# One product of each expert layer by seven products of quarters, with sums accumulated in PSUM

## The chip, the cores and the metric

The kernel runs on one core of a Trainium2 chip. The metric is the device time of one execution in microseconds; the median of three runs counts.

## What is computed

The reference is an attention block followed by a mixture of experts. The first half gives, for 8 batches and 8 heads of 576 positions and width 64, a softmax over the scores that lie within tau of the row's maximum, times v. Its output is 4608 token rows of 512 numbers. The second half sends each token to one of 8 experts by a hash of its id:

```python
expert_idx = token_ids * np.int64(2654435761) % np.int64(E)
for e in range(E):
    mask = expert_idx == e
    xe = x[mask]
    h = np.maximum(xe @ w1[e], 0.0)
    out[mask] = h @ w2[e]
```

w1[e] is 512 x 1024, w2[e] is 1024 x 512; all is fp32.

## The kernel before

**Stages.** The attention stage takes about the first half of the time. While it runs, the tokens are ranked by expert, and x is written to a scratch tensor in DRAM (x_scratch). The experts follow, in the order of their token counts, 0 to 7. The slots of an expert are 544 (expert 0), 576 (1 to 4) or 600 (5 to 7); slots beyond that go to a loop for the overflow, which has nothing to do here. Expert 0's first layer is done plainly during attention's end (`early_h`, `late_h`); the change does not touch it.

**One expert.** All operands stand transposed: h = relu(w1^T x) has features on the partitions and tokens as columns. A layer is one matrix product a b, where a is the weight (the stationary operand) and b the activations (the moving one). Both are cut into 2 x 2 blocks, and the four blocks of the result are made by seven products in Winograd's form, not eight (`seven`, L926): with sums s2, s3, s4 (and s1, in place of a21) of the blocks of a, and t2, t3, t4 (and t1, in place of b12) of those of b,

- p1 = a11 b11, and c11 = p1 + a12 b21
- u2 = p1 + s2 t2, u3 = u2 + s3 t3, c21 = u3 + a22 t4
- k5 = s1 t1, u4 = u2 + k5, c22 = u3 + k5, c12 = u4 + s4 b22

A product is 2 output blocks of 128 features by n_k chunks of 128 inner elements, with half the tokens as columns (272, 288 or 300; 240 in expert 7's second layer, whose last 120 slots `last_tile` does, L983). In layer 1 n_k is 2, and the block of a is done in two groups of columns, so it has 14 products of 4 matmuls (`layer1`, L963); in layer 2 n_k is 4 and there are 7 products of 8 matmuls (`layer2`, L972). Each product has a PSUM tile of its own; four tiles go round (`bank2`, L851, tiles sc and bank2). Each of the sums u2, u3, u4 and each output block is an add on DVE (L861) from PSUM to SBUF; p1 is copied by ACT (L951), and in layer 1 ACT applies relu to each output block (L948).

**Weights of layer 2.** For experts 0 to 6 the columns of w2 are dealt: output feature 4 m + i is row m of block i (`dealt`, L877; `w2_blocks`, L880). So a weight load from w_sb in layer 2 takes every fourth word of a row; one from the sums w2_s takes every second. Expert 7 takes them as they stand. The dealt order lets DVE transpose the output in 32 x 32 squares (`put_squares`, L1024), which POOL then scatters to the output in DRAM (L1036).

**The order of the work.** Both expert blocks are under `manual_schedule`: the engines run what the code emits, in that order. `seven` calls a function after each step (`side1` in layer 1, `side2` in layer 2), which emits the work for what comes next. In layer 1 of expert e these are the sums of w2 (`sums_w2`), the second half of the previous expert's squares, the first half of the sums of h, and the squares of the next expert's x (`turn_x`, L1052, with 16 transfers xT<-xq on SP's queue, L1064). In layer 2 they are the sums of the next expert's w1 and x, the gathers of x for expert e + 2 (`fetch`, on POOL), the load of w1 for expert e + 2 (on SP), and the first half of the squares. For expert 0 all of the next expert's x is turned in its layer 2.

Of the kernel before, what the change touches and what calls it, by code (L numbers as in the profile page):

```python
# [20 lines left out]
def kernel(  # L21
# [805 lines left out]
    with tc.tile_pool(name="m_x", bufs=1) as m_x, \  # L827
         tc.tile_pool(name="m_o", bufs=3) as m_o, \
         tc.tile_pool(name="m_s", bufs=1) as m_s:
# [7 lines left out]
        nc.gpsimd.memset(oT[:, :, CAP:SL], 0.0)  # L837
        o_end = m_x.tile([P, DIN], FP32, name="o_end")
        mark = m_x.tile([P, 1], FP32, name="mark")
# [4 lines left out]
        h_s = m_s.tile([P, 3, FH, CH], FP32, name="h_s")  # L844
        halves = [m_s.tile([P, 2, CH], FP32, name=n) for n in ("p1", "u2", "u3", "u4")]
        CHL = 32 * (NB - 4) // 2

        ps_m = ctx.enter_context(tc.tile_pool(name="ps_m", bufs=2, space=PSUM))
        turn = [0]

        def bank2():  # L851
            turn[0] ^= 1
            if turn[0]:
                return ps_sc.tile([P, 2, 512], FP32, name="sc")
            return ps_m.tile([P, 2, 512], FP32, name="bank2")

# [52 lines left out]
        def sums_w2(e):  # L909
            s1 = None  # L910
            if e == E - 1:
                spare = w_pool.tile([P, CO, F], FP32, name="w1_sb")
                s1 = w_tiles["s1"] = spare[:, :, 0:D2]
            return left(*w2_blocks(e, w_tiles[e, 2]), w2_sums(e), s1)

# [9 lines left out]

        def seven(a, a_s, b, b_s, m0, outs, relu, after):  # L926

            (a11, a12, s1, a22), (s2, s3, s4) = a, a_s
            (b11, t1, b21, b22), (t2, t3, t4) = b, b_s
            c11, c12, c21, c22 = outs  # L930
            n_k, width, dealt_out = a11.shape[1], b11.shape[2], len(a11.shape) == 4
            p1, u2, u3, u4 = (t[:, :, 0:width] for t in halves)

            def product(x, y):
                ps = bank2()
                for i in range(2):
                    c0 = m0 + P * i
                    for c in range(n_k):
                        lhsT = (x[:, c, :, i] if dealt_out else
                                x[:, c, c0:c0 + P])  # L940
                        nc.tensor.matmul(ps[:, i, 0:width], lhsT=lhsT, rhs=y[:, c],  # L941
                                         start=c == 0, stop=c == n_k - 1)
                return ps[:, :, 0:width]

            def out(c, ps, u, step):
                add(c, ps, u)()
                if relu:
                    nc.scalar.activation(c, c, AF.Relu)  # L948
                after(step)

            nc.scalar.copy(p1, product(a11, b11))  # L951
            out(c11, product(a12, b21), p1, 0)
            add(u2, product(s2, t2), p1)()
            after(1)
            add(u3, product(s3, t3), u2)()
            after(2)
            out(c21, product(a22, t4), u3, 3)
            k5 = product(s1, t1)
            add(u4, k5, u2)()
            out(c22, k5, u3, 4)  # L960
            out(c12, product(s4, b22), u4, 5)

        def layer1(e, side):  # L963

            w, half = w_tiles.pop((e, 1)), caps[e] // 2
            for g in range(NG):
                outs = [h_0[:, FH * i + 2 * g:FH * i + 2 * g + 2, half * k:half * k + half]
                        for i in range(2) for k in range(2)]
                seven(w1_blocks(w), triple(w1_s, 0, C2), x_blocks(e), triple(x_s, 0, C2, half), 2 * P * g,
                      outs, True, lambda step: side(g, step))  # L970

        def layer2(e, side):  # L972

            w, half = w_tiles[e, 2], half2(e)
            outs = [oT[:, C2 * i:C2 * i + C2, half * k:half * k + half]
                    for i in range(2) for k in range(2)]
            a = w2_blocks(e, w)
            if e == E - 1:
                a[2] = w_tiles["s1"]
            seven(a, w2_sums(e), h_blocks(0, FH, half),  # L980
                  triple(h_s, 0, FH, half), 0, outs, False, side)

        def last_tile(middle):  # L983

            w, o_sb, idx = w_tiles[E - 1, 2], o_end, gidx[:, KT - 1:KT]
            rows = CAP - 2 * CHL
            for c0, c1 in ((0, DIN - P), (DIN - P, DIN)):
                ps = bank2()
                for fo in range(FO):
                    nc.tensor.matmul(ps[0:rows, 0, 0:c1 - c0], lhsT=h_0[:, fo, 2 * CHL:CAP],  # L990
                                     rhs=w[:, fo, c0:c1], start=fo == 0, stop=fo == FO - 1)
                    if (c0, fo) == (0, FH - 1):
                        middle()
                nc.scalar.copy(o_sb[0:rows, c0:c1], ps[0:rows, 0, 0:c1 - c0])
            put_rows(o_sb[0:rows], idx[0:rows])

        def put_out(e, *groups):
# [14 lines left out]
            for tr, kts in zip(trs, groups):  # L1012
                for i, kt in enumerate(kts):
                    rows = rows_of(kt)
                    o_sb = m_o.tile([P, DIN], FP32, name="o_sb")
                    dst = o_sb[0:rows].rearrange("p (c r q) -> p r c q", c=CO, r=2)
# [52 lines left out]
        with tc.manual_schedule():  # L1069
            run(sums_w2(0), 4)  # L1070
            fill(18)
            late_h(lambda fo: (ps_sc.tile([P, 2, 512], FP32, name="sc") if fo in (2, 4) else
                               ps_m.tile([P, 2, 512], FP32, name="bank2")))
            fetch(1)
            run(sums_h(0, 0, FH), 4)

        with tc.manual_schedule():
            for e in range(E):
                more = e + 1 < E
                turns = turn_x(e + 1) if more else []  # L1080

                if e > 0:
                    w2_work, h_work = sums_w2(e), sums_h(e, 0, 2)

                    def side1(g, step):
                        if g == 0:
                            run(w2_work)
                            if step == 0:
                                put_squares(e - 1, 1)
                        else:  # L1090
                            run(h_work)
                        if step > 2:
                            run(turns, 1 if g == 0 else 2)

                    layer1(e, side1)
                    run(sums_h(e, 2, FH), 4)
                x_work = (sums_w1(e + 1) + sums_x(e + 1)) if more else []

                def side2(step):
                    if step == 0:  # L1100
                        run(turns, len(turns))
                    else:
                        run(x_work, 2)
                    if step == 2 and e + 2 < E:
                        fetch(e + 2)
                    if step == 4 and e + 2 < E:
                        load_w1(e + 2)
                    if more and step == 3:
                        put_squares(e, 0)
# [23 lines left out]
        with tc.For_i(0, n_ov, 1) as it:  # L1133
# [23 lines left out]
            for fo in range(FO):  # L1157
                nc.tensor.matmul(o_ps[:, 0], lhsT=h_0[:, fo, 0:P], rhs=w2_sb[:, fo],
                                 start=(fo == 0), stop=(fo == FO - 1))
            o_sb = m_o.tile([P, DIN], FP32, name="o_sb")  # L1160
            nc.scalar.copy(o_sb[:], o_ps[:, 0])
# [35 lines left out]
```

## Time and profile before

| | |
|---|---|
| median of three runs | 918.71 us (918.48 to 920.31) |
| the profiled execution, its own time | 931.3 us |
| its span, first to last instruction | 929.7 us |
| experts, from expert 0's second layer | 501 to 930 us |
| expert 0, layer 2, on TensorE | 501.0 to 527.0 us |
| expert 1, layers 1 and 2 | 527.0 to 583.3 us |
| expert 7, layer 1 to the last product | 861.3 to 914 us |

In a line of instructions by time: start and length in us, engine (PE is TensorE's matmuls, PEld its weight loads, DVE VectorE, ACT ScalarE, POOL GpSimd, SPq SyncE's queue), line of the kernel, operation, output<-inputs by the names of their tiles (without numbers), the shape (partitions x columns, or active rows*columns of the array and the size of the moving operand), and the count of instructions that were merged into the line. In brackets is the idle time before it and who ended that. Matmuls overlap, so a matmul's length is more than the distance to the next one's start. In a list by source the three numbers are the shortest, the median and the longest duration in ns. In a list of waits they are the sum in us, the number of waits and the longest one.

### The profile page before, as it was taken

Reading aid. Unit: us, or ns where it says so; the run is one execution under the profiler, and the core shown is the slowest. Engines: PE = TensorE matmul, PEld = TensorE weight load, DVE = VectorE, ACT = ScalarE, POOL = GpSimd, SP = SyncE. Lnnn points to the kernel's source line nnn. Section 1 sums busy time; section 2 is a strip of 40 time slices with the busy share of each in tenths; the row PEclk is TensorE's granted clock in tenths of the full one; section 3 lists DMA queues with packets and bytes.
Section 4 is the critical chain, followed back from the end, with each engine's and each line's share of the span. In section 5 each row is a group of like instructions: output and inputs, shape, how many; then the busy total and the mean of one; then the engine's idle time right before and its main releaser. Section 6 shows DMA issues by size and latency. Waiting matters only on the chain.

```text
span 929.7 us, 20725 instructions
## 1 busy us (share of the span) xinstructions
PE 909.8 (98%) x7495; PEld 662.0 (71%) x7495; DVE 757.5 (81%) x1654; ACT 457.3 (49%) x741; POOL 403.7 (43%) x528
## 2 busy tenths in 40 slices
PE   7999999999999999999999999999999999999996
PEld 4666666656666566665678888788887978878785
DVE  7999999999999999999955776767668676777551
ACT  6888888888888898888812010110201021020110
POOL 4232432456666623455423370724527073440702
PEclk9999999999999999999999999999999999999999
DMA  7354463554545668743101745364372536412101
GB/s 175 92 148 118 109 152 93 136 131 103 123 105 153 159 165 214 216 107 88 30 25 51 237 131 158 133 173 141 95 223 75 164 133 165 157 34 50 48 3 55
DMA packets 114775, 113.11 MB, mean 122 GB/s; under 512 B 32475, under 2 KB 89315, under 8 KB 114672
## 3 DMA queue, kind: packets, MB, share of 16 engines
q1 hardware_dynamic: 105168, 92.64, 37.0%
q0 software_dynamic: 9072, 18.91, 7.0%
q8 instruction: 61, 1.00, 0.4%
q14 instruction: 42, 0.34, 0.1%
q10 hardware_dynamic: 432, 0.21, 0.1%
HBM read 81.99 MB, written 21.44 MB: 111 GB/s over the span
## 4 chain that ended last, share of the span: by engine, by line
PE 65%; issue 21%; POOL 7%; DVE 3%; ACT 2%; DMA 1%; another core or an unknown queue 1%; POOLq 0%; SPq 0%; DVEq 0%; ACTq 0%
PE av L313 18%; PE sc L235 15%; PE tr L282 11%; PE sc L941 9%; PE bank L941 8%; POOL out_dram L1036 6%; PE sc L640 2%; PE av L282 1%; POOL xg L119 1%; ACT w L260 1%; DVE ns L246 1%; DVE w L271 1%; ACT wT_b L303 1%; ACT wT_a L303 0%
## 5 line engine op out<-in xcount | busy, mean ns | idle before, releaser
L260 ACT ACTIVATE w<-ns,nmx 128x576 f32<-128x576 f32 x288 | 220.5, 777 | 28.8 <-DVE ns L246 27.8
L271 DVE SCALAR_TENSOR_TENSOR w<-ns,thr,w 128x576 f32<-128x576 f32 x288 | 225.8, 816 | 0.0
L1036 POOL DMA_INDIRECT out_dram<-o_q,qidx x127 | 138.1, 1087 | 191.7 <-DVE o_q L1028 153.1
L246 DVE TENSOR_SCALAR_CACHE_REDUCE ns<-sc 128x576 f32<-128x576 f32 x288 | 205.6, 747 | 8.1 <-PE sc L235 7.4
L253 POOL TENSOR_SCALAR thr<-nmx,drop 128x2 f32<-128x2 f32 (+1 forms) x160 | 104.4, 653 | 187.3 <-DVE ns L246 177.6
L235 PE MATMUL sc<-k_sb,q 64*128 64x288 f32 (+1 forms) x1280 | 179.2, 423 | 1.0 <-DVE drop L704 0.7
L282 PEld LDWEIGHTS tr<-ident,w 64*128 64x128 f32 x2624 | 106.0, 138 | 95.4 <-ACT wT_b L303 32.4
L282 PE MATMUL tr<-ident,w 64*128 64x64 f32 x2624 | 139.5, 231 | 6.0 <-ACT wT_b L303 2.6
L948 ACT ACTIVATE h<-h 128x576 f32<-128x576 f32 (+1 forms) x56 | 38.7, 693 | 164.8 <-DVE h L861 126.1
L235 PEld LDWEIGHTS sc<-k_sb,q 64*128 64x128 f32 (+1 forms) x1280 | 93.0, 177 | 23.2 <-DVE ns L246 9.4
L313 PE MATMUL av<-wT_a,v 128*64 128x320 f32 (+1 forms) x704 | 100.6, 418 | 0.2
L303 ACT COPY wT_a<-tr 128x512 f32<-128x512 f32 (+1 forms) x128 | 81.7, 638 | 20.7 <-PE tr L282 20.2
L303 ACT COPY wT_b<-tr 128x512 f32<-128x512 f32 (+1 forms) x128 | 81.4, 636 | 17.1 <-PE tr L282 11.2
L313 PE MATMUL av<-wT_b,v 128*64 128x256 f32 x640 | 83.2, 389 | 0.0
L313 PEld LDWEIGHTS av<-wT_a,v 128*64 128x64 f32 x704 | 43.8, 137 | 29.3 <-DVE xm L352 0.7
L951 ACT COPY p<-bank 128x576 f32<-128x576 f32 (+2 forms) x11 | 7.0, 633 | 99.5 <-PE bank L941 72.5
L313 PEld LDWEIGHTS av<-wT_b,v 128*64 128x64 f32 x640 | 40.2, 136 | 18.8 <-issue 0.7
L542 POOL DMA_INDIRECT slot_scratch<-tok,slot_i x36 | 45.0, 1251 | 9.4 <-issue 7.6
L941 PE MATMUL bank<-h,w_sb 128*128 128x288 f32 (+3 forms) x192 | 48.1, 404 | 0.0
L941 PE MATMUL sc<-h,w_sb 128*128 128x288 f32 (+3 forms) x192 | 47.7, 401 | 0.0
L941 PEld LDWEIGHTS bank<-h,w_sb 128*128 128x128 f32 x192 | 46.6, 300 | 0.5
L941 PEld LDWEIGHTS sc<-h,w_sb 128*128 128x128 f32 x192 | 45.9, 289 | 0.6
(197 smaller groups left out, 1303.7 us busy)
## 6 DMA issues: line engine op xcount, KB each, us to landing
w_sb<-in_moe_w_dram SPq DMA_DIRECT2D x16, 2048.0 KB
q<-in_q_dram SPq DMA_DIRECT2D x62, 288.0 KB
v<-in_v_dram SPq DMA_DIRECT2D x32, 256.0 KB
x_scratch<-xm SPq DMA_DIRECT2D x32, 256.0 KB
xT<-xq SPq DMA_DIRECT2D x84, 80.0 KB
k_sb<-in_k_dram SPq DMA_DIRECT2D x31, 144.0 KB
k_sb<-in_k_dram SPq DMA_DIRECT2D x32, 112.0 KB
x_scratch<-xg SPq DMA_DIRECT2D x9, 256.0 KB
```

The source lines that it names most:

```text
L235: nc.tensor.matmul(sc[out_rows, i, 0:S2], lhsT=q_sb[rows, h, q0:q1], rhs=k_sb[rows, h], start=True, stop=True)
L246: nc.vector.tensor_scalar(out=ns[:].rearrange("p (i s) -> p i s", i=2), in0=sc[:, :, 0:S2], scalar1=-1.0, scalar2=None, op0=ALU.mult, op1= ...
L253: nc.gpsimd.tensor_scalar(out=thr[:, 0:j + 1], in0=stats[n][0][:, 0:j + 1], scalar1=drop[:], scalar2=None, op0=ALU.add)
L260: nc.scalar.activation(w, nss[n, j][:], AF.Exp, bias=stats[n][0][:, j:j + 1], scale=-1.0)
L271: nc.vector.scalar_tensor_tensor(out=w, in0=nss.pop((n, j))[:], scalar=stats[n][1][:, j:j + 1], in1=w, op0=ALU.is_le, op1=ALU.mult, accum_ ...
L282: nc.tensor.transpose(dst[:, r, 64 * c:64 * c + 64], src[rows, c0:c0 + P], ident[rows, rows])
L303: nc.scalar.copy(dst, tr[:, :, 0:64 * n_c].rearrange("p r (c q) -> p r c q", c=n_c))
L313: nc.tensor.matmul(av[64 * j:64 * j + 64, g, c0:c1], lhsT=v_sb[:, c, 64 * j:64 * j + 64], rhs=wT[g][:, i, c0:c1], start=(c == 0), stop=stop)
L542: nc.gpsimd.indirect_dma_start(out=slot_dram[c % 2][:, :], out_offset=bass.IndirectOffsetOnAxis(ap=slot_i[:, c:c + 1], axis=0), in_=tok[:, ...
L941: nc.tensor.matmul(ps[:, i, 0:width], lhsT=lhsT, rhs=y[:, c], start=c == 0, stop=c == n_k - 1)
L948: nc.scalar.activation(c, c, AF.Relu)
L1036: inst = nc.gpsimd.indirect_dma_start(out=rows[:, :], out_offset=bass.IndirectOffsetOnAxis(ap=idx, axis=0), in_=o_sb, in_offset=None, boun ...
```

## The change

From expert 1 on, the product a12 b21 of each layer (in layer 1 for both groups of columns at once) is done by the same seven-product form on quarters: a12 and b21 are cut into 2 x 2, with half the inner chunks, half the output blocks and half the tokens (144, 150 or 120 columns) each. A product of quarters is 2 matmuls; there are seven, so 14 half-width matmuls stand in place of 8. Their blocks of a are taken straight from the weight tile (in layer 2 in the dealt order), with s1 in place, or from a new tile wi_s of contiguous sums; those of b from xT or h, with t1 in place, or from bi_s. Their results go to the output block c11, to which p1 is added.

The sums u2, u3 and u4 are no longer adds on DVE. Products accumulate in PSUM: x holds p1, then u2, u3 and c21; z holds k5, then k5 + s4 b22. At each stage ACT copies what is needed later (p1, u2, and k5 or u3), and the DVE adds left are c11, c22 and c12. Between two products of one accumulation another one stands. The four PSUM tiles are now taken once and kept (`banks`). The same form holds for expert 0's second layer, but with a12 b21 whole.

The order of the side work moves: 16 inner sums are added to it; the squares of the next x move from both groups of layer 1 to the second; the first half of the output squares moves from step 3 to step 4 of layer 2, behind the sums of x; `put_out` for expert 7's first tile goes between the two halves of its last product. The tiles for output rows (o_sb, o_end) are now those of the gathered x.

The core of the diff, with the new functions:

```diff
-        halves = [m_s.tile([P, 2, CH], FP32, name=n) for n in ("p1", "u2", "u3", "u4")]
+        halves = [m_s.tile([P, 2, CH], FP32, name=n) for n in ("p1", "u2", "u3")]
+        wi_s = m_s.tile([P, 3, D2], FP32, name="wi_s")
+        bi_s = m_s.tile([P, 3, CH], FP32, name="bi_s")
+        quarters = [m_s.tile([P, CH], FP32, name=n) for n in ("q_p1", "q_u2", "q_p5")]
...
+        def bank2():
+            turn[0] += 1
+            return banks[(turn[0] - 1) % 4]
...
+        def products(ps, x, y, start, mid=None):
+
+            for i, lhsTs in enumerate(x):
+                for c, lhsT in enumerate(lhsTs):
+                    nc.tensor.matmul(ps[:, i], lhsT=lhsT, rhs=y[:, c], start=start and c == 0,
+                                     stop=c == len(lhsTs) - 1, skip_group_check=not start)
+                if i == 0 and mid:
+                    mid()
...
+        class Seven:
...
+            def first(self):
+                products(self.x, self.a[0], self.b[0], True)
+
+            def keep_p1(self):
+                nc.scalar.copy(self.p1, self.x)
...
+            def u2_sum(self):
+                products(self.x, self.a[4], self.b[4], False)
+                nc.scalar.copy(self.u2, self.x)
+
+            def s1_t1(self, keep):
+                products(self.z, self.a[2], self.b[1], True)
+                if keep:
+                    nc.scalar.copy(self.mid, self.z)
+
+            def u3_sum(self, keep):
+                products(self.x, self.a[5], self.b[5], False)
+                if keep:
+                    nc.scalar.copy(self.mid, self.x)
+
+            def c21(self):
+                products(self.x, self.a[3], self.b[6], False)
...
+            def c12(self, mid=None):
+                products(self.z, self.a[6], self.b[3], False, mid)
+                self.out(self.outs[1], self.z, self.u2)
...
+        class Quarters:
...
+            def p1_p2(self):
+                products(self.x, self.a[0], self.b[0], True)
+                nc.scalar.copy(self.p1, self.x)
+                products(self.y, self.a[1], self.b[2], True)
...
+            def p5_u2(self):
+                products(self.z, self.a[2], self.b[1], True)
+                nc.scalar.copy(self.p5, self.z)
+                products(self.x, self.a[4], self.b[4], False)
+                nc.scalar.copy(self.u2, self.x)
+
+            def c12_c22(self):
+                products(self.z, self.a[6], self.b[3], False)
+                add(self.outs[1], self.z, self.u2)()
+                products(self.x, self.a[5], self.b[5], False)
+                add(self.outs[3], self.x, self.p5)()
+
+            def c21(self):
+                products(self.x, self.a[3], self.b[6], False)
+                nc.scalar.copy(self.outs[2], self.x)
...
+        def w_quarters(a):
+
+            if len(a.shape) == 4:
+                return [a[:, 2 * j:2 * j + 2, :, i:i + 1] for i in range(2) for j in range(2)]
...
+            g0.first()
+            g0.keep_p1()
+            side(0)
+            q.p1_p2()
+            q.c11()
+            g0.u2_sum()
+            side(1)
+            q.p5_u2()
+            g0.s1_t1(True)
+            side(2)
+            q.c12_c22()
+            side(3)
+            g0.u3_sum(False)
+            q.c21()
+            g0.c22(g0.x)
+            side(4)
+            g0.c12()
+            g0.c11(g0.p1)
+            g1.first()
...
+            g1.u2_sum()
+            side(7)
+            g1.s1_t1(True)
+            side(8)
+            g1.u3_sum(False)
+            side(9)
+            g1.c22(g1.x)
+            g1.c12()
+            g1.relus()
+            side(10)
+            g1.c21()
...
+            if e == 0:
+                o.second(banks[2])
+                side(0)
+                o.u2_sum()
+                side(1)
+                o.s1_t1(True)
+                side(2)
+                o.u3_sum(False)
+                o.c22(o.x)
+                side(3)
+                o.c12()
+                o.c21()
+                side(4)
+                return
+            q = quarters_of(e, 2, banks[2][:, 0:1], banks[2][:, 1:2], banks[3][:, 0:1])
+            q.p1_p2()
+            q.c11()
+            run(inner_b(second_blocks(e, 2)[1]), 4)
+            o.u2_sum()
+            q.p5_u2()
+            side(0)
+            o.u3_sum(True)
+            side(1)
+            q.c12_c22()
+            o.s1_t1(False)
+            side(2)
+            q.c21()
+            o.c11(o.p1)
+            o.c22(o.z)
+            o.c21()
+            side(3)
+            o.c12(lambda: side(4))
...
-            w, o_sb, idx = w_tiles[E - 1, 2], o_end, gidx[:, KT - 1:KT]
+            w, o_sb, idx = w_tiles[E - 1, 2], xg_bufs[KT - 1], gidx[:, KT - 1:KT]
...
+                    def side1(step):
+                        if step == 0:
+                            put_squares(e - 1, 1)
+                        run(w2_work, (0, 1, 2, 1, 2, 1, 1, 0, 0, 0, 0)[step])
+                        run(h_work, 2 if step in (8, 9) else 0)
+                        run(turns, (0, 0, 0, 0, 0, 0, 1, 2, 1, 1, 1)[step])
...
+                x_work = []
+                if more:
+                    x_work = sums_w1(e + 1) + sums_x(e + 1)
+                    a, b = second_blocks(e + 1, 1)
+                    x_work += inner_w(a) + inner_b(b)
...
                 def side2(step):
                     if step == 0:
                         run(turns, len(turns))
-                    else:
-                        run(x_work, 2)
+                    run(x_work, (1, 2, 3, 10, 0)[step])
                     if step == 2 and e + 2 < E:
                         fetch(e + 2)
                     if step == 4 and e + 2 < E:
                         load_w1(e + 2)
-                    if more and step == 3:
+                    if more and step == 4:
                         put_squares(e, 0)
```

## The prediction

> **What bounds the kernel now.** I read the page first (busy shares and slices), then the windows of the expert stage, then TensorE's timeline and the durations of its weight loads, then the waits.
>
> ```profile
> PE 909.8 (98%) x7495; PEld 662.0 (71%) x7495; DVE 757.5 (81%) x1654; ACT 457.3 (49%) x741; POOL 403.7 (43%) x528
> PE   7999999999999999999999999999999999999996
> ```
>
> ```profile
> 501.00:527.00 26.00, 26.00 (x114) 24.38 (x114) 18.68 (x22) 1.93 (x3) 9.84 (x10) 1.00 0.52 137
> 527.00:911.00 384.00, 380.51 (x1562) 317.88 (x1561) 271.07 (x326) 51.29 (x78) 163.41 (x152) 1.00 0.39 121
> ```
>
> A windows line gives length, then busy time of PE, PEld, DVE, ACT and POOL. From 501 us (expert 0's second layer) to 911 us TensorE is never idle but for 3.5 us; DVE is busy 71%, ACT 13%, at full clock. TensorE is the bound, and it is bound in a measurable way: by the pace at which matmuls start. A program's fp32 matmul is two matmul records, each with its own weight load (112 matmuls an expert in the code, some 224 records in 54.4 us). I call one record a pass.
>
> ```profile
> 641.49 2.10 PE L941 MATMUL bank<-x_s,w_s 128*128 128x288 f32 x8
> 643.43 2.10 PE L941 MATMUL sc<-x_s,w_s 128*128 128x288 f32 x8
> ...
> 920.41 1.91 PE L990 MATMUL sc<-w_sb,h 128*120 128x128 f32 x16
> ```
>
> Eight passes of 288 columns start 1.94 us apart: 0.2425 us each. The row of 16 passes of 128 columns: 1.91 less one record of 0.273, over 15: 0.109. In the same way 240 columns take 0.2025 (890.91 to 894.15 us for 16) and 300 take 0.2525. On this line 144 columns take 0.1225, 150 take 0.1275.
>
> **Where the pace is not the columns.** Expert 0's second layer has 272 columns throughout, but two paces:
>
> ```profile
> 501.02 3.90 PE L941 MATMUL sc<-h,w_sb 128*128 128x272 f32 x16
> 504.76 3.90 PE L941 MATMUL bank<-h,w_sb 128*128 128x272 f32 x16
> 508.49 3.83 PE L941 MATMUL sc<-h_s,w_s 128*128 128x272 f32 x16
> 512.16 3.83 PE L941 MATMUL bank<-h_s,w_s 128*128 128x272 f32 x16
> ```
>
> ```profile
> L941 PEld LDWEIGHTS bank<-h,w_sb x32: 316/316/321, 504.5 to 522.8; 128*128 128x128 f32 x32
> L941 PEld LDWEIGHTS sc<-h_s,w_s x16: 195/196/201, 508.3 to 511.7; 128*128 128x128 f32 x16
> ```
>
> From w_sb 16 passes take 3.735 us (0.2335 each), from w_s 3.67 (0.2295, the line above). The weights of w_sb are "dealt": a column is every fourth fp32 word, 16 bytes apart; those of w_s every second. The dealt load lasts 316 ns against 196, and the matmuls then start at its pace, not at theirs. With 288 columns (0.2425) it just hides.
>
> [...]
>
> **Part 1, layer 1's quarters (experts 1 to 7).** Removed: a12 b21 of two groups, 8 matmuls, 16 passes of 288: 3.88 us (300: 4.04). Added: seven products of 2 matmuls of half the columns, 28 passes. Weights here (w1_sb, wi_s) are contiguous: 28 x 0.1225 = 3.43 (3.57). Gain 0.45 to 0.47; times 7: -3.2 us, all on the path.
>
> **Part 2, layer 2's quarters, experts 1 to 6.** Removed again 16 passes, 3.88 (4.04). Of the added 28 the products with a11, a12, s1 and a22 take dealt weights.[...] In the order of the built program: p1 and p2 are 8 passes, 7 followed by a dealt load; p5 4, 3 of them; c12 and c22 8, the last (before s1 t1); c21 4, all. So 15 intervals of 0.2335 and 13 of 0.1225: 3.50 + 1.59 = 5.09 us. Loss 1.21 (at 300 columns 5.16 - 4.04 = 1.12): 4 x 1.21 + 2 x 1.12 = +7.1 us. The trace shows no dealt load beside so narrow a matmul; bounds are hidden (0.1225) and the whole load (0.316), which the starts 0.2335 apart at 272 columns exclude[...]. I take 0.2335, since it already sets the pace there.
> Expert 7's w2 is not dealt: 28 passes of 120 columns[...]: 3.05 against 16 x 0.2025 = 3.24: -0.2.
>
> **Part 3, accumulating in PSUM.** The number of whole products stays. What is new is that x or z may not be accumulated into until ACT or DVE has read it, with one product between.
>
> - Expert 0, layer 2. The order is p1, a12 b21, u2, s1 t1, u3, c12, c21. Product c21 accumulates into the bank that c22's add on DVE reads. That add stands behind two x sums, which wait for expert 1's turned tokens:
>
> ```profile
> 512.62 10.66 SPq L1064 DMA_DIRECT2D xT<-xq  x16
> ```
>
> ```profile
> 524.76 0.76 DVE L858 TENSOR_TENSOR x_s<-xT 128x576 f32<-128x576 f32 x1 [4.27 <-DMA xT<-xq]
> 525.55 0.76 DVE L858 TENSOR_TENSOR xT<-xT 128x576 f32<-128x576 f32 x1
> ```
>
> The squares ahead of these 16 DMAs keep their place, so the two sums end where they do now and the next DVE instruction starts at 526.2; c22's add (0.72) ends at 526.95, TensorE restarts at 527.1. Its c12 ends at 501.0 + 5 or so products = 523.25 (the whole 25.96 less one of 3.74). Pause: +3.9 us. Now four banks in turn hide this wait; the cover is gone.
> - Last tile. It takes the bank of c12, which DVE must have read: record end 0.16 after the pace, 0.07 to DVE, 0.66 (480 elements), 0.15 to restart: +1.05 us. Before, nothing waits there.
> - Layer 1's u2 waits for ACT's copy of p1 (626 ns): 0.16 + 0.06 + 0.63 + 0.05 + 0.1 to 0.2 for the load = 1.0 to 1.1, cover 8 x 0.1225 = 0.98. 0.05 to 0.1 each, with two such in expert 7: +0.7. Elsewhere the cover is 1.3 us (u2 to u3 in layer 2) or a whole product: 0.
>
> **Part 4, the rest.** DVE loses 12 adds of 750 ns an expert and gains six quarter adds and 16 inner sums of 144 to 288 elements (0.3 to 0.45 by the rows of 480 to 1088): 15.8 us becomes about 15.5. ACT gains some 5 us on an engine busy 13%. The first output transpose moves behind x's sums, and its nine POOL scatters some 4 us later; POOL is busy 163 of 384. The squares move into group 1, their 16 SP transfers still start some 20 us before x's sums of experts 2 to 7. The w loads behind them stay. Output tiles in xg_bufs, free by then: 0. If DVE should be late, the next thing late is TensorE at the same accumulations.
>
> Sum: -3.2 + 7.1 - 0.2 + 3.9 + 1.05 + 0.7 = +9.3 us. On the profiled execution (span 929.7, its own time 931.3) that is 940.6; the runs' median is 918.7, 12.6 below, and I carry the microseconds over: **928.0 us**.
>
> **Rivals.**
>
> - The pauses of before go. TensorE idles 3.5 us in six pauses, with 0.16 tail and 0.1 restart each about 5:
>
> ```profile
> PE bank L941 <- DVE h_s L858: 1.9, 2, 1.6
> PE sc L941 <- ACT p L951: 0.6, 1, 0.6
> ```
>
> For it: fewer DVE adds stand between a product and a free bank. Against: DVE and ACT started late there although the product had ended. 928.0 - 5.1 = 922.9.
> - More pauses: the same late starts, of 2 to 5 us, meet one product of cover (1.9 us in group 1) where four banks stood. As much again: 933.
> - Not slower: the dealt load hides under the narrow matmul[...]. Then 15 intervals fall from 0.2335 to 0.1225 or 0.1275, 1.6 us in six experts: -9.9, so 918.1; with the pauses gone too, 913. It decides at an interval of 131 ns.[...]
> - The change does less than it says (DVE relief with no effect): it is in the sum, at 0.
>
> **Chances.** Sum as worked out 0.52 (925.5 to 930.5); pauses go 0.17; more pauses 0.17; load hidden 0.14, half of it with the pauses gone. Range 922 to 933: the pauses either way[...]; out of it stay the last case and some of the third. Measurable is about 0.2% (1.8 us): slower 0.86, same 0.07, faster 0.07.
>
> **What would show it.** Rows of 144-column passes starting 0.12 us apart in layer 1 and 0.23 in layer 2; a TensorE pause of nearly 4 us before expert 0's last product, released by DVE, and of 1 us before the last tile. Wrong would make it dealt passes below 0.13, or turned tokens that land by 521.

## The result and the profile after

| | before | changed |
|---|---|---|
| median (four runs each) | 918.6 us (918.2 to 920.3) | 935.2 us (934.3 to 936.6) |
| ratio, 95% interval | | 1.0179 [1.0161, 1.0197] |
| profiled execution, its own time | 931.3 us | 936.6 us |
| span | 929.7 us | 935.0 us |

The change costs 16.6 us; the forecast was 9.3 us, and 935.2 lies above the range of 922 to 933.

The two profiles on hand then can't simply be subtracted, since the one of before is of an execution 12.6 us above its median. A profile of before taken later (own time 919.9, span 918.3) mends that. It is compared here with one of the changed kernel from a second execution (own time 934.9, span 933.3). Each number is the distance in us between the starts of TensorE's first matmuls of two stages, rounded by itself:

| stage | before | changed | difference | forecast |
|---|---|---|---|---|
| up to expert 0's layer 2 | 493.2 | 492.9 | -0.3 | 0 |
| expert 0, layer 2 | 26.0 | 33.4 | +7.4 | +3.9 |
| expert 1, layer 1 | 28.8 | 26.9 | -1.9 | -0.4 |
| experts 2 to 7, layer 1 | 166.3 | 163.6 | -2.7 | -2.1 |
| experts 1 to 6, layer 2 | 165.2 | 176.1 | +10.9 | +7.1 |
| expert 7, layer 2 to the last tile | 23.3 | 24.8 | +1.5 | +0.8 |
| the rest | 15.5 | 15.6 | +0.1 | 0 |
| span | 918.3 | 933.3 | +15.0 | +9.3 |

The spans differ by 15.0 us and the medians by 16.6, because this execution of before lies 1.2 us above its median and that of the changed kernel 0.3 below.

Where did the excess come from? TensorE's waits, from expert 0's second layer on, in the changed kernel's profile (sum in us, number, longest):

```profile
PE sc L935 <- DVE oT L865: 3.6, 1, 3.6
PE sc L935 <- ACT q_p L1018: 2.6, 7, 0.4
PE bank L1187 <- DVE oT L865: 0.8, 1, 0.8
PE sc L935 <- ACT oT L994: 0.7, 1, 0.7
```

The first and third were forecast. The second was not, and its 0.4 is less than it costs, as the timeline of ACT and TensorE at the start of expert 1's second layer shows:

```profile
559.80 0.28 ACT L1018 COPY q_p<-sc 128x144 f32<-128x144 f32 x1 [0.18 <-PE sc L935]
```

```profile
554.90 4.86 PE L935 MATMUL sc<-h,w_sb 128*128 128x288 f32 x20
560.13 1.21 PE L935 MATMUL sc<-h,w_sb 128*128 128x144 f32 x4 [0.37 <-ACT q_p L1018]
```

The 20 passes are the 16 of the first product and the 4 of the quarters' p1. Then p2 waits until ACT has copied p1, though it goes to the other half of the tile (`banks[2][:, 1:2]` beside `banks[2][:, 0:1]`). From p1's last start to p2's first are 0.643 us more than a 144-column pass takes, and the next start is late by another 0.226: the weight loads were held as well, and the first behind the wait began at 560.13, 0.57 us after the one before it had ended.

The timelines of TensorE and DVE at the end of expert 0:

```profile
520.37 6.94 PE L935 MATMUL sc<-h_s,w_sb 128*128 128x272 f32 x16 [3.59 <-DVE oT L865]
528.02 2.21 PE L935 MATMUL sc<-xT,w_sb 128*128 128x288 f32 x8 [0.70 <-ACT oT L994]
```

```profile
518.13 0.76 DVE L862 TENSOR_TENSOR x_s<-xT 128x576 f32<-128x576 f32 x1 [7.40 <-DMA xT<-xq]
...
519.60 0.72 DVE L865 TENSOR_TENSOR oT<-sc,u 128x544 f32<-128x544 f32 x1
```

As forecast, c22's add (519.60) stands behind two x sums that waited for the turned tokens, and TensorE pauses 3.76 us for it. But then the same 16 passes that took 3.90 us take 6.94. The windows show why; the column after the five engines' busy times is the granted clock:

```profile
516.00:520.30 4.30, 0.78 (x4) 0.32 (x2) 2.13 (x4) 0.00 (x0) 0.00 (x0) 0.92 0.47 118
520.30:524.00 3.70, 3.63 (x8) 2.81 (x9) 3.53 (x9) 0.00 (x0) 0.00 (x0) 0.50 1.02 419
```

TensorE ran at half clock from 519.64 us for 6.83 us. The clock fell 2.9 us after the end (516.78) of the last matmul before the pause, and it came back 6.1 us after the restart. Here the passes start 0.453 apart, not 0.2335: +3.05 us. On top, c21 is now last and stands in bank 0, where expert 1's first product must wait for ACT's copy of it (528.02): 0.86.

### The profile page after: what moved, and what is told of

It is laid out like the page before. It is cut to its first block, busy times and chain, and to the rows that moved or that the text cites. A ratio compares the mean times of both kernels' runs of the same rounds, so it can differ in the third digit from the quotient of the medians.

```text
span 935.0 us, 21277 instructions
## 1 busy us (share of the span) xinstructions
PE 915.2 (98%) x7663; PEld 675.1 (72%) x7663; DVE 760.9 (81%) x1720; ACT 503.5 (54%) x842; POOL 409.5 (44%) x528
## 4 chain that ended last, share of the span: by engine, by line
PE 77%; issue 12%; POOL 4%; ACT 2%; DMA 2%; DVE 2%; SPq 1%; POOLq 0%; DVEq 0%; ACTq 0%
PE av L313 18%; PE sc L935 17%; PE sc L235 15%; PE bank L935 12%; PE tr L282 10%; POOL out_dram L1233 4%; PE sc L640 2%; PE av L282 1%; ACT w L260 1%; DMA xT<-xq 1%; DMA k_sb<-in_k_dram 1%; DVE ns L246 1%; SPq L1261 0%; PE bank L658 0%; PE sc L658 0%
## 5 line engine op out<-in xcount | busy, mean ns | idle before, releaser
L935 PE MATMUL sc<-h_s,w_s 128*128 128x288 f32 (+3 forms) x256 | 63.7, 402 | 0.0
L935 PEld LDWEIGHTS sc<-h_s,w_s 128*128 128x128 f32 x256 | 49.1, 196 | 9.7
L542 POOL DMA_INDIRECT slot_scratch<-tok,slot_i x36 | 48.0, 1332 | 10.1 <-issue 7.4
L935 PE MATMUL sc<-h,w_sb 128*128 128x288 f32 (+6 forms) x200 | 49.0, 396 | 2.6 <-ACT q_p L1018 2.6
L959 ACT ACTIVATE h<-h 128x576 f32<-128x576 f32 (+1 forms) x42 | 29.0, 693 | 40.6 <-DVE h L865 40.6
L119 POOL DMA_INDIRECT xg<-x_scratch,gidx_x x35 | 38.5, 1099 | 15.2 <-issue 6.1
```

The costliest lines, as they stand in the source:

```text
L119: nc.gpsimd.indirect_dma_start(out=dst, out_offset=None, in_=src, in_offset=bass.IndirectOffsetOnAxis(ap=idx, axis=0), bounds_check=src.sh ...
L542: nc.gpsimd.indirect_dma_start(out=slot_dram[c % 2][:, :], out_offset=bass.IndirectOffsetOnAxis(ap=slot_i[:, c:c + 1], axis=0), in_=tok[:, ...
L935: nc.tensor.matmul(ps[:, i], lhsT=lhsT, rhs=y[:, c], start=start and c == 0, stop=c == len(lhsTs) - 1, skip_group_check=not start)
```

## The theory, and its rivals

Theory: beside the forecast terms there are three steady costs that it lacked: the half clock after the pause (3.05), expert 1's first product waiting for c21 (0.86), and p2's wait for p1 (0.643 + 0.226 - 0.11, the slow interval that it hides: 0.76 an expert; the runs below give 0.65, since it hides two slow intervals). The dealt quarter weights cost what was forecast. Rivals: the half clock comes from the work or from a timetable and not from the pause; the passes after the pause are slow because of the DMA traffic beside them (419 GB/s in the window above); p2's wait hides dealt loads, so that nothing is won by removing it; accumulating in PSUM costs by itself; the narrow passes are held by something other than their dealt weights.

## The experiments

### First set: one wait at a time, on another chip

These four runs fell on a chip where the kernel before takes 938.1 us (932.6 to 940.6), for a reason of which part is shown below, so only single stages are read from them.

**The kernel before, unchanged.**

> The kernel before, unchanged, for a second trace. If the profiled execution of before was late for reasons of its own (attention's end at 501 us, six TensorE pauses among the experts), this one has expert 0's second layer start near 494 us, as the changed kernel's does, few pauses, and a span near 917 us. If those belong to the kernel, they come again at a span near 930 us.

It took 937.2 us with the longest wait of TensorE 2.7 us, "issue" (nothing recorded). Expert 0's layer 2 began only at 502.2 us, 9 later than in the later profile of before. The late begin and the pauses came again, but on this chip they don't tell whether they belong to the kernel; the third set does.

**The x sums behind c22's add, in expert 0 alone.**

```diff
-                    run(x_work, (1, 2, 3, 10, 0)[step])
+                    run(x_work, ((1, 2, 3, 10, 0) if e > 0 else (1, 2, 1, 12, 0))[step])
```

> The changed kernel, with expert 0's x sums put behind c22's add on DVE. Theory (a pause, and a half clock that follows from it): the pause of 3.8 us and the 3.0 us that the half clock adds both go; 935.2 becomes about 928.4, the clock stays at 1.0 through 528 us, and the wait of some 0.8 us before expert 1's first product stays. Rival (the last product is slow because the weight load of 2 MB runs beside it at 419 GB/s): only the pause goes, about 931.5.

In all 1002.0 us, ratio 1.063 [1.059, 1.067]. Expert 0's second layer, however, took 26.8 us at full clock. TensorE's timeline there, to be read beside that of the changed kernel above:

```profile
524.42 3.90 PE L935 MATMUL sc<-h_s,w_sb 128*128 128x272 f32 x16
529.02 1.24 PE L935 MATMUL sc<-xT,w_sb 128*128 128x288 f32 x4 [0.70 <-ACT oT L994]
```

Pause and half clock are gone; the wait for c21 has stayed. The total can't tell the two expectations apart on this chip.

**One more product in the pause** (s2 t2 into a free bank, its result not used).

```diff
                 o.c12()
+                products(banks[3][:, :, 0:half], o.a[4], o.b[4], True)
                 o.c21()
```

> The changed kernel with one more product on TensorE in expert 0's pause: u2's s2 t2 once more, into a bank that nobody reads, so TensorE works through the wait and DVE's order is untouched. Theory (clock): c21 still starts at about the same time, but at full pace, 3.7 us for its 16 matmul records instead of 6.6: about 932. Rival (memory traffic beside it): c21 keeps its slow pace, and the time stays at 935.2.

1005.8 us, ratio 1.069 [1.064, 1.074]; expert 0's second layer 31.0 us at full clock. It is repeated below.

**p2 of layer 2 in another tile.**

```diff
-            q = quarters_of(e, 2, banks[2][:, 0:1], banks[2][:, 1:2], banks[3][:, 0:1])
+            q = quarters_of(e, 2, banks[2][:, 0:1], banks[3][:, 1:2], banks[3][:, 0:1])
```

> The changed kernel with the quarter product p2 of layer 2 in another PSUM tile than p1. Theory (p2 waits for ACT's copy of p1 because both lie in one tile): the wait of some 0.76 us in experts 1 to 6 and 0.5 in expert 7 goes, 935.2 becomes about 930.2. Rival (p2 waits for its operand, the relu of the last block of layer 1): no change, 935.2.

1004.7 us, ratio 1.071 [1.067, 1.075]. Two second layers took 28.4 us undisturbed, the first here as a window, against 29.0 us for two of the kernel with the x sums moved, on the same chip:

```profile
633.00:661.40 28.40, 28.40 (x126) 26.16 (x126) 18.57 (x30) 4.33 (x9) 0.00 (x0) 1.00 0.46 133
```

The wait is worth 0.6 us an expert, and removing it wins that.

**Why these three lose 64 to 68 us against before.** From the kernel with the x sums moved, SP's queue, TensorE and DVE:

```profile
554.32 10.72 SPq L1261 DMA_DIRECT2D xT<-xq  x16
```

```profile
554.40 2.10 PE L935 MATMUL bank<-xT,w_s 128*128 128x288 f32 x8
560.26 4.21 PE L935 MATMUL bank<-x_s,w_sb 128*128 128x288 f32 x8 [3.75 <-issue]
```

```profile
559.44 0.76 DVE L865 TENSOR_TENSOR h<-bank,u 128x576 f32<-128x576 f32 x1 [5.18 <-remote]
```

The product before 554.40 had ended at 554.57, but DVE's add of it started only at 559.44, 4.87 us later. No other input of the add was late (ACT had copied u by 553.4). That TensorE's signal reached DVE late is an inference from this; just then the 16 transfers xT<-xq ran. TensorE had one product of cover, paused 3.75 us, and went on at half clock (8 passes in 4.21 us). "remote" means that the profile shows no instruction that ended the wait. On this chip DVE and ACT wait so many times in an execution (here DVE 47.9 us in eleven waits, ACT 43.8 in four); the first profile of before has such waits too (DVE 10.0 us in four), while the profiles from the other chips, the later one of before and those of the changed kernel included, have none among the experts. The kernel before, with four tiles in turn, takes about 19 us more on this chip, of which some 9 come ahead of the experts; the kernels with accumulation lose 64 to 68 more than it. That is the rival "more pauses" of the forecast, which does not occur on the chip of the result. The changed kernel itself was not run on this chip, and what delays these adds and copies stays open.

### Second set: all four waits, then the dealt weights, then layer 1 alone

This and the third set are from chips where the kernel before takes 918.7 and 918.8 us.

**The changed kernel again.**

> The changed kernel once more, as the reference of this set. Theory (the time is made of steady costs: dealt quarter passes, expert 0's pause with its half clock, the wait of p2): 935 us again, expert 0's layer 2 33.6 us, the layers 2 of experts 1 to 4 29.0 us. Rival (the changed order is exposed to late signals of TensorE, as the runs of the first set were on another chip): 950 us and more here too, through pauses of 4 us and over in many stages, each followed by half clock; then only single undisturbed stages can be read.

934.97 us, ratio 1.0184 [1.0167, 1.0201]; the costs are steady.

**Four waits taken away.**

```diff
-                      False, banks[0], banks[1])
+                      False, *(banks[0:2] if e > 0 else banks[2:4]))
...
-                o.second(banks[2])
+                o.second(banks[0])
...
-            q = quarters_of(e, 2, banks[2][:, 0:1], banks[2][:, 1:2], banks[3][:, 0:1])
+            q = quarters_of(e, 2, banks[2][:, 0:1], banks[3][:, 1:2], banks[3][:, 0:1])
...
             rows = CAP - 2 * CHL
+            turn[0] += 1
...
-                    run(x_work, (1, 2, 3, 10, 0)[step])
+                    run(x_work, ((1, 2, 3, 10, 0) if e > 0 else (1, 2, 1, 12, 0))[step])
```

> Four changes that take waits away: expert 1's x sums stand behind expert 0's c22 add; expert 0's second layer uses banks 2 and 3 so that expert 1's first product finds bank 0 free; p2 of layer 2 goes to a tile of its own; the last tile skips the bank of c12. Theory: expert 0's layer 2 falls from 33.6 to 26.0 us with no half clock (-3.76 pause, -3.05 clock, -0.86 the wait of expert 1), the layers 2 of experts 1 to 4 from 29.0 to 28.4 (-0.62 as in one undisturbed stage of the first set), all in all -4.4, the tail -1.0: 935.2 - 13.1 = 922.1, still slower than before by the dealt quarters. Rival 1 (p2's wait covers dealt loads that then show): layer 2 stays at 29.0, 926.5. Rival 2 (half clock comes from work, not from the pause): expert 0 falls by 4.6 only, 925.1.

926.4 us, ratio 1.0085 [1.0068, 1.0101]. The total is the number of rival 1, and its reason is nevertheless wrong. The windows are expert 0's layer 2 and expert 1's layers 1 and 2:

```profile
492.90:518.90 26.00, 26.00 (x114) 24.38 (x114) 17.28 (x20) 3.15 (x5) 10.30 (x10) 1.00 0.55 137
518.90:550.40 31.50, 28.72 (x126) 22.86 (x125) 26.92 (x40) 9.87 (x17) 19.60 (x18) 0.95 0.48 168
550.40:578.70 28.30, 28.30 (x125) 26.10 (x125) 18.47 (x30) 4.32 (x9) 4.34 (x5) 1.00 0.60 165
```

Expert 0 fell to 26.0 and the second layers of experts 1 to 4 to 28.4 (by the starts of their first matmuls), both as the theory has it. But expert 1's first layer rose from 26.9 to 31.5: the pause moved on. DVE and TensorE there:

```profile
522.67 0.72 DVE L865 TENSOR_TENSOR oT<-bank,u 128x544 f32<-128x544 f32 x1
523.30 4.06 DVE L1226 STREAM_TRANSPOSE o_q<-oT 128x1024 f32<-128x1024 f32 x2
527.20 0.45 DVE L865 TENSOR_TENSOR h<-sc,q_p 128x288 f32<-128x288 f32 x1
```

```profile
524.28 0.65 PE L935 MATMUL bank<-bi_s,wi_s 128*128 128x144 f32 x4
527.71 3.90 PE L935 MATMUL sc<-xT,w_sb 128*128 128x288 f32 x8 [2.78 <-DVE h L865]
```

TensorE arrives 7.4 us earlier and meets the work that DVE did under the old pause: sums, then two output transposes of 4.06 us, and only then the quarters' c11 add, which frees the tile. 2.78 us of pause, and 3.4 us at half clock (+1.8).

**The quarter weights of layer 2 laid side by side.** On top of the four edits, a11, a12 and a22 of the quarters are copied by ACT, and s1 is written by DVE, into the dead a12 block of w1's tile.

```diff
+        def packed(e):
+            w = w_tiles[e, "dead"]
+            return [w[:, C2 + i // 2, D2 * (i % 2):D2 * (i % 2) + D2].rearrange("p (k m i) -> p k m i", k=2, i=1)
+                    for i in range(4)]
+
+        def pack(e, a):
+            return [lambda i=i: nc.scalar.copy(packed(e)[i], w_quarters(a)[i]) for i in (0, 1, 3)]
...
+            elif layer == 2:
+                a_q = packed(e)
...
+                        run(c_work, 1 if step in (6, 7, 8) else 0)
```

> As the kernel with four waits taken away, and the quarter weights of layer 2 (a11, a12, a22 by ACT's copies, s1 by DVE's sum) are laid contiguously into the dead a12 block of w1's tile. Theory (the dealt loads set the pace of the narrow passes): 15 intervals of 0.2335 become 0.1225 in each of experts 1 to 6, layer 2 falls from 28.4 to 26.7 us (from 29.4 to 27.8 at 300 columns), 922.1 - 9.8 = 912.3 us, faster than before. Rival (the narrow passes are held by something else, such as the change of bank or the waits between short products): under 3 us, 919 to 922.

918.95 us, ratio 1.0003 [0.9994, 1.0012]; less than the kernel before it by 7.45, not 9.8 (the pause in expert 1 is in both). In the profiles the six second layers fall by 1.3 us each. The same layer, TensorE's rows without packing and with it:

```profile
559.88 0.98 PE L935 MATMUL bank<-h,w_sb 128*128 128x144 f32 x4
...
561.19 4.04 PE L935 MATMUL sc<-h_s,w_s 128*128 128x288 f32 x16
```

```profile
559.55 0.65 PE L935 MATMUL bank<-h,w_sb 128*128 128x144 f32 x4
...
560.53 4.12 PE L935 MATMUL sc<-h_s,w_s 128*128 128x288 f32 x16
```

p5's four passes fall from 0.98 to 0.65 us, three intervals of 0.111 us less; all narrow passes now start 0.1225 apart. What the expectation missed: two of the 15 slow intervals belong to the dealt load of a wide product behind a narrow one (the quarters' c22 to s1 t1, the quarters' c21 to c21), and stay. Two more appear, before s3 t3 (4.12 against 4.04 above) and s2 t2, 0.08 and 0.02. 13 x 0.111 - 0.10 = 1.34, and the layer fell from 28.36 to 27.03.

**Quarters in layer 1 alone** (the four edits, but a12 b21 of layer 2 whole, with the order of expert 0, and no inner sums of w2 and h).

```diff
-            if e == 0:
-                o.second(banks[0])
+            if True:
+                o.second(banks[0] if e == 0 else banks[2])
...
-                    w2_work += inner_w(a, None if more else w_tiles["s1_q"])
```

> As the kernel with four waits taken away, but the quarters stay in layer 1 alone: in layer 2 of every expert a12 b21 is done whole, and the inner sums of w2 and h are left out. Theory: layer 2 costs 27.16 us at 288 columns and 28.28 at 300 as before the change, -1.2 x 4 - 1.1 x 2 + 0.2 = -6.9 against the kernel with the quarters: 915.2 us; against before that leaves layer 1's -3.2 alone: 918.6 - 3.2 = 915.4. Rival (accumulating in PSUM costs by itself, through waits with one product of cover): 918 to 925, with waits of TensorE for DVE or ACT in layer 2.

927.3 us, ratio 1.0097 [1.008, 1.0114]: a miss, and not for the rival's reason. TensorE's two longest waits from expert 0's second layer on:

```profile
PE sc L935 <- ACT oT L994: 4.4, 6, 0.7
PE sc L935 <- DVE h L865: 2.9, 1, 2.9
```

In this order c21 is the last product and lies in bank 0, where the next expert begins: 0.9 us, six times, and the last transposes wait for it too. With the moved pause (expert 1's first layer 31.7 us) that is 11 of the 12 us of excess.

### Third set: the moved pause, and before without disturbance

**Before, for its profile.**

> The kernel before, unchanged, for a profile of an execution near its median. Theory: its span is some 917 us, expert 0's second layer begins at 493 to 494 us as in the changed kernel, and most of the six TensorE pauses of the first profile (501.0, span 929.7) are absent: they belonged to that execution. Rival: the pauses are in every execution, and the median lies at 918.7 by an earlier begin alone; then the changed kernel gained them.

Span 918.3, expert 0's layer 2 at 493.2 us. The six pauses of the first profile are absent. There is one other, in expert 1's first layer, which takes 28.8 us instead of 27.2; none follows:

```profile
PE bank L941 <- DVE x_s L858: 1.4, 1, 1.4
```

**The best version.** The packed kernel; DVE does the inner sums of w1 while it waits for the tokens, and expert 0's output squares behind the quarters' adds of expert 1.

```diff
                     x_work += inner_w(a) + inner_b(b)
+                    if e == 0:
+                        x_work[4:12] = x_work[8:12] + x_work[4:8]
...
-                        if step == 0:
+                        if step == (0 if e > 1 else 5):
                             put_squares(e - 1, 1)
+                        if step == 3 and e == 1:
+                            put_squares(0, 0)
...
-                    if more and step == 4:
+                    if more and step == 4 and e > 0:
                         put_squares(e, 0)
```

> As the kernel with four waits taken away and packed quarter weights, and the DVE order between expert 0 and 1 is mended: the inner sums of w1 stand ahead of the x sums, expert 0's output squares (4.06 us) behind two adds of expert 1's first layer. Theory: the pause of 2.78 us there, and the half clock after it (+1.9), go: expert 1's first layer 26.7 instead of 31.4 us, 918.95 - 4.7 = 914.3 us, ratio to before 0.995. Rival (the pause moves on once more, to the adds that now stand ahead of or behind the squares): 916 to 919 with another pause in expert 1.

915.5 us (915.4 to 915.8), ratio 0.9964 [0.9951, 0.9978]: faster than both kernels. Windows of expert 1's two layers:

```profile
519.10:547.40 28.30, 27.22 (x126) 21.64 (x125) 25.24 (x36) 11.49 (x20) 13.23 (x12) 1.00 0.47 170
547.40:574.40 27.00, 27.00 (x125) 24.59 (x125) 18.41 (x30) 4.13 (x9) 10.54 (x11) 1.00 0.61 180
```

The half clock is gone, and of the pause 1.25 us is left (1.08 idle, the rest the last matmul's end), now before a product of the second group, which waits for an add behind the second square:

```profile
534.03 2.29 DVE L1236 STREAM_TRANSPOSE o_q<-oT 128x1152 f32<-128x1152 f32 x1
536.62 0.76 DVE L865 TENSOR_TENSOR h<-bank,h 128x576 f32<-128x576 f32 x1
```

```profile
537.43 2.21 PE L935 MATMUL bank<-x_s,w_s 128*128 128x288 f32 x8 [1.08 <-DVE h L865]
```

So the expectation was 1.2 us too low, and its rival half right.

**Quarters in layer 1 alone, mended** (the same DVE edits; `*banks[2:4]` for all experts' layer 2; the last tile takes its bank as in the changed kernel).

```diff
-                      False, *(banks[0:2] if e > 0 else banks[2:4]))
+                      False, *banks[2:4])
...
-                o.second(banks[0] if e == 0 else banks[2])
+                o.second(banks[0])
```

> Quarters in layer 1 alone, as in the run of that kind before, with the DVE order between expert 0 and 1 mended, and with layer 2 of all experts on banks 2 and 3, so that c21, which is last, does not hold bank 0 for the next expert's first product. Theory (accumulating in PSUM costs nothing but such waits): 927.3 - 6 x 0.9 - 4.7 = 917.2, of which 0.8 is the last transposes' wait for c21; ratio to before 0.998. Rival (it costs more by itself): waits of TensorE in layer 2 of 0.3 us and more remain, 919 or more.

917.2 us, ratio 0.9982 [0.9975, 0.9988], as the theory has it. The second layers of experts 1 to 4 take 27.16 us, as before the change: accumulating costs nothing where no wait shows.

**The filled pause again.** The edit of the first set.

> The changed kernel with one extra product (s2 t2, its result not used) in expert 0's pause. Theory (the half clock follows from the idle time): no half clock up to 530 us, expert 0's second layer 30.5 us instead of 33.5. In total less: TensorE then meets DVE's output squares in expert 1, whose end does not move, a pause of up to 2.2 us; 932 to 934.2. Rival (half clock comes on a timetable of its own or from the work): 33.5 + some, 935 to 938.

932.9 us, ratio 1.0152 [1.0136, 1.0167]. TensorE at the end of expert 0 (the first row is the added product), and the window of c21:

```profile
516.24 3.83 PE L935 MATMUL bank<-h_s,w_s 128*128 128x272 f32 x16
520.42 4.13 PE L935 MATMUL sc<-h_s,w_sb 128*128 128x272 f32 x16 [0.35 <-DVE oT L865]
525.25 2.21 PE L935 MATMUL sc<-xT,w_sb 128*128 128x288 f32 x8 [0.70 <-ACT oT L994]
```

```profile
520.40:524.20 3.80, 3.78 (x16) 3.78 (x16) 3.59 (x9) 0.00 (x0) 0.00 (x0) 1.00 1.01 417
```

With more work in it the kernel is 2.1 us faster: c21's 16 passes, which begin at the same time as in the changed kernel (520.4), take 4.13 us instead of 6.94, at full clock. The stage is 31.2 us and not 30.5, since c22's add is still waited for and c21's first two starts come 0.7 us late. The DMA traffic beside c21 is the same (417 against 419 GB/s), so it isn't what slowed the passes: without the idle time the clock stays whole. Of the pause of up to 2.2 us that was feared in expert 1 nothing came (26.9 us).

## Why the prediction was wrong, by its own steps

Two steps failed, both in Part 3: the term of expert 0 was mis-sized (+3.9, measured +7.4), and "Elsewhere ... 0" left out a wait that costs 4.5 us. All the signs that the prediction named came true, but they tested only the terms that it had.

- **What bounds the kernel now** held: TensorE by the starts of its passes. The profiled execution did not stand for the median: its late begin (501.0 against 493.2) and its six pauses are not in an undisturbed execution. Carrying only the sum of microseconds over to 918.7 was right all the same; the rival "the pauses of before go" had nothing to take but the 1.6 us of expert 1, which are indeed gone (the -1.9 in the table).
- **Part 1** (-3.2): right. Layer 1 takes 26.7 for 27.2 and 27.8 for 28.3, -0.4 to -0.5 each.
- **Part 2** (+7.1): right. With p2's wait away the layers 2 of experts 1 to 6 sum to 172.2 us against 165.2: +7.0. There are 15 slow intervals in each, as counted, 0.10 to 0.11 us slow each, though two of them lie behind the first pass of a wide product (in c21 of expert 1 the starts at 576.04 and 576.39 are 0.354 apart, not 0.2425). The count gave each slow interval to the load that follows, which was the author's estimate; in the trace the slow ones lie one pass later: p5's first interval in expert 1, beside a dealt load of 309 ns, is 0.123 us, and its last, beside a contiguous one of 208 ns, 0.233. The -0.2 of expert 7 came to 0 (23.26 us up to the last tile with the waits taken away, 23.27 before). That its passes of 120 columns keep the 0.109 of the row of 128 was an estimate too; the last three intervals of p2 there are 0.111 to 0.112. The rival "load hidden" fell: it decided at 131 ns, and they are 0.2335.
- **Part 3, expert 0** (+3.9): the mechanism and the pause were right (3.76), the size of the stage was not (+7.4). The term took TensorE to restart at its old pace, and gave no reason for it. Missing were the half clock that the pause brings on (+3.05 in the first profile; in that of the table the pause is 3.97 and the half clock costs 2.6), shown by the filled pause, and expert 1's first product behind c21's copy (+0.87, gone with other banks).
- **Part 3, "Elsewhere the cover is 1.3 us (u2 to u3 in layer 2) or a whole product: 0"**: this step failed. Between the quarters' p1 and p2 there is no product at all. They are two halves of one tile, and the second waits for the copy out of the first: 0.65 us in each of experts 1 to 6 (28.36 against 29.01 at 288 columns), 0.6 in expert 7 (21.1 against 21.7), in all 4.5 us. The step looked for waits between products of one accumulation, not between tiles shared for another reason.
- **Part 3, last tile** (+1.05): right, 0.91 measured (the last half product to the last tile takes 2.64 us, and 1.73 when the bank is skipped); **layer 1's u2** (+0.7): no wait is listed, 0.
- **Part 4** (0): right; no other wait of TensorE is listed.
- **More pauses** (933): on the chip of the result none came. The near 935 is not this rival's doing.

Sum of the misses: 3.5 (expert 0) + 4.5 (p2) - 0.7 (u2) - 1.6 (the pause of before) = 5.7; with the 9.3 of the forecast that is 15.0, the difference of the two spans. Smaller differences, none over 0.3, cancel.

## What to carry to other kernels

A pause of TensorE is to be priced with what follows it: here 2.78 and 3.59 us idle cost another 1.8 and 3.05 us at half clock, so filling the longer one with useless work paid. When a wait is removed, ask what the waiting engine will meet next: the work that hid under the pause (here DVE's output squares) is the next wait, and a total that fits the rival's number may still have another cause. And accumulating in PSUM in place of adds cost nothing itself here (27.16 us a second layer with and without it), but it took away the slack of a rotation of tiles (3.76 us at c22's add): list for each tile who reads it last, its two halves and its next user in the following stage included.

## What had not been expected of the hardware

- On one of the chips used, DVE and ACT started late beside the 16 transfers of SP's queue, the add above 4.87 us after the product that it reads had ended, for a cause that stays open. The kernel with four tiles in turn took 19 us more on that chip, those with one product of cover 64 to 68 more than it.
- The length of a pause alone did not decide on the half clock here. It came with the pause of 3.59 us idle in the changed kernel, for 6.83 us, and after 2.78 us idle in the kernel with four waits removed, for 3.4 us. After 1.44 us (before) and 1.08 us (the best version) it did not come. But in the first set, in the kernel with the x sums moved, 1.99 us idle was followed by it and 3.46 us was not (two restarts, and the windows behind them with the granted clock):

```profile
807.72 0.78 PE L935 MATMUL bank<-bi_s,w_sb 128*128 128x150 f32 x4 [1.99 <-DVE h L865]
...
881.83 2.29 PE L935 MATMUL bank<-xT,w_sb 128*128 128x300 f32 x8 [3.46 <-ACT h L1038]
```

```profile
808.60:812.00 3.40, 3.40 (x8) 1.97 (x6) 0.20 (x1) 0.00 (x0) 2.73 (x3) 0.50 0.18 58
...
881.90:886.10 4.20, 4.20 (x16) 2.88 (x16) 1.85 (x3) 1.51 (x3) 3.29 (x4) 1.00 0.21 66
```

The clock record of that trace shows more. Its half clocks among the experts begin at 559.41, 614.02, 699.36, 747.14, 808.59, 815.41 and 890.50 us, which are 16, 25, 14, 18, 2 and 22 times 3.413 us apart. In the profile of the changed kernel the half clock lasts from 519.64 to 526.47 us, 2 times 3.413, and the next begins at 932.65, 119 times 3.413 later; in the first profile of before one lasts from 17.99 to 21.40 us, once 3.413. So the recorded changes of the clock lie on marks 3.413 us apart. The pause of 1.99 us (805.73 to 807.72) lies between two such marks, that of 3.46 us (878.37 to 881.83) across one (880.26). That where a pause falls counts too is a guess from these two; what decides stays open.
